# Attention and feed-forward in one kernel: shifted exponent patterns made by 64-bit additions on GpSimd, some pairs of them summed on VectorE, and an opening that gives GpSimd's work to others while a library is loaded

## The chip, the cores and the metric

The kernel runs on one core of a Trainium2 chip. The metric is the device time of one execution in microseconds (us). Three runs of the kernel before took 705.05, 705.12 and 705.44 us; the median is 705.12 us. The engines are called PE (TensorE), ACT (ScalarE), DVE (VectorE), POOL (GpSimd) and SP (SyncE, which issues most DMAs).

## The reference

With x of 2048 rows by 640, 32 heads of width 20 that share one K and one V, and a feed-forward width of 1536:

```python
xn = layernorm(x)
q = (xn @ wq) as 32 heads of 20;  k = xn @ wk;  v = xn @ wv        # k, v: 2048 x 20
A = concat_heads(softmax(q @ k.T * 20**-0.5) @ v) @ wo
B = square(relu(xn @ w1 + b1)) @ w2 + b2
out = x + A + B
```

All inputs and the output are bf16.

## The kernel before, in words

**Tiles.** The attention is cut into 32 blocks: 4 groups of 512 query rows times 8 groups of 4 heads. A block has 16 key tiles of 128 rows. A score tile is 128 keys by 512 queries of one head, so there are 32 x 16 x 4 = 2048 score tiles. One matmul of depth 20 makes one of them in a bank of PSUM (`QK..` and `DQK..`, "ps<-qT,kT" in the profile); up to four matmuls of different heads run side by side in four row groups of the array. The exponential then turns it into bf16, and a group of four matmuls, one for each head (`PV..`, `DPV..`), multiplies it with the tile of V and a column of ones and adds it up in bank 7.

**Two ways to an exponential.** ACT does the exact one: one ACTIVATE (`make_act`, L910) takes two neighbouring banks, sometimes three, into the ring `PT`. The other way is a *set*: four score tiles (the four heads) of one key tile. DVE turns each of the four into a bf16 pattern by one multiplication and addition that is written as a 16-bit integer (`D1_..`, L1083), which is a straight line in place of the exponential between powers of two. Three shifted copies of the 128x2048 pattern are made by adding 32, 64 and 96 to its 16-bit integers (`P1..P3`, the *passes*, L1101), and the four patterns go through V with the weights `TW` (0.84, 0.71, 0.59 for the shifted ones, in the tiles `vxs`), so that the four lines average to a good exponential. This takes four matmul groups in place of one. A pass runs on POOL or on DVE, by a rule in `after_dqk` that compares how far the two queues reach.

**Around it.** The rest is units of matmuls on PE with an evacuation each: transposes of xn (`unit_T`), K, V and Q, the two feed-forward layers, and the output projection. Normalising the attention goes through DRAM by DMAs that SP issues.

**The opening.** Eight DMAs on SP's queue and four on ACT's load x, wk, wv and the first columns of wq. Each group of 128 rows of x (`rows(st)`) gets its mean and variance on DVE (two BATCH_NORM_STATS2) or ACT, the inverse root on POOL (`PW..`, L434, a power of -0.5) and the normalised rows (`XN..`, L436) on DVE or POOL. PE transposes the first four groups with the identity matrix `ident` (L475), ACT moves them to SBUF (`TE..`, L477), PE makes K, Q and V of them, and the first ACTIVATE of L910 follows. POOL builds `ident` by a select (L373).

**What sets the order.** A planner in the Python of the kernel runs before the program is built. It keeps a clock for each engine, gives each operation a duration written in the code, and commits one operation after the other, by priorities that `RULES` changes for stages of 10 us. Its result is one fixed list for each engine with semaphore waits; nothing is decided on the chip. Operations marked `lock=True` (the passes, `SQ`, `CM`, `XN` and others, in SBUF alone) are planned so that one on DVE and one on POOL do not overlap, and a POOL operation of this kind waits for the last such DVE operation ahead of it. How many score tiles go each way comes out of the planner: 1480 go through ACT (665 ACTIVATEs of two, 50 of three) and 568 through 142 sets.

Of the kernel before, what the change touches and what calls it, by code (L numbers as in the profile page):

```python
# [8 lines left out]
U16 = mybir.dt.uint16  # L9
ALU = mybir.AluOpType  # L10
# [22 lines left out]
TW = [1.0, 0.83984375, 0.70703125, 0.59375]  # L33


def _pl(z):
# [17 lines left out]
JIT = 0.8  # L54
# [6 lines left out]
DLAST = 7.5  # L61
DSLACK = 0
URG = 4.0
PBIAS = 0.6
DGAP = 0.5
# [7 lines left out]
            xc=[f"FE{24 + k}" for k in range(8)] + [f"RL0_{k}" for k in range(4)] + ["RL3_0", "RL3_1", "RL3_1", "RL3_2"],  # L73
            xb=[f"RL0_{k}" for k in range(6)] + ["RL3_3", "RL3_5"])
# [4 lines left out]
ACTEV = (0, 2)  # L79
KEEP = 1  # L80
RULES = {3: {'PVA': 2.1, 'PVD': 2.1, 'R3': 1, 'PP': 0.9},
         4: {'PVA': 2.1, 'PVD': 2.1, 'R3': 1, 'PP': 0.9, 'WARM': 0.78},
         5: {'D1P': 1, 'MPRIO': 0.5, 'PBIAS': 2.5},
         6: {'D1P': 1, 'MPRIO': 0.5, 'PBIAS': 2.5, 'ND': 1, 'QKP': 0},
         7: {'DQP': 2.05, 'URG': 2, 'PVD': 2.1, 'BEHIND': -0.3},
         8: {'WARM': 0.85, 'DQP': 0.95},
         10: {'ND': 1, 'NOPEN': 3},
         11: {'ND': 1, 'NOPEN': 3},
         12: {'EPS': 0.12},
         13: {'EPS': 0.06, 'EVP': 0.3},  # L90
         15: {'PBIAS': 0},
         17: {'EPS': 0.06},
         18: {'EPS': 0.12},
         19: {'WARM': 0.78, 'PBIAS': 2.5, 'IDLE': 0.3},
         21: {'PBIAS': 0, 'KEEP': 0},
         23: {'EPS': 0.12},
         25: {'R3': 1, 'EVP': 0.3},
         26: {'R3': 1, 'EVP': 0.3, 'IDLE': 0.3, 'PVD': 2.1},
         28: {'EPS': 0.12, 'URG': 3},
         29: {'EPS': 0.12, 'URG': 3, 'KEEP': 3, 'EVP': 1.1, 'ND': 3},  # L100
         31: {'PBIAS': 1, 'D1P': 1, 'PVD': 1.05},
         32: {'PBIAS': 1, 'D1P': 1, 'PVD': 1.05, 'DGAP': 0.8, 'DQP': 0.95, 'SQP': 2, 'R3': 1},
         36: {'PP': 0.9, 'BEHIND': -0.1, 'EVP': 0.3, 'PBIAS': 1.5},
         37: {'URG': 3, 'JIT': 1.0, 'PVD': 1},
         38: {'SQP': 0.7, 'URG': 3},
         39: {'PP': 2.5},
         40: {'PBIAS': 1},
         41: {'PBIAS': 1, 'DGAP': 1.5, 'SQP': 0.7},
         42: {'PBIAS': 1, 'DGAP': 1.5, 'SQP': 2, 'NOPEN': 3, 'ND': 2, 'PVD': 1},
         43: {'PBIAS': 1, 'DGAP': 1.5, 'SQP': 2, 'NOPEN': 3, 'ND': 2, 'PVD': 1, 'R3': 9},  # L110
         44: {'WARM': 0.78, 'KEEP': 3, 'DLAST': 7.5},
         45: {'DGAP': 0.8, 'KEEP': 1, 'D1P': 3},
         48: {'PBIAS': 1},
         49: {'PBIAS': 1, 'R3': 1},
         50: {'PBIAS': 1, 'R3': 1},
         53: {'DLAST': 3.5},
         54: {'DLAST': 3.5, 'EPS': 0, 'EVP': 0.3},
         55: {'DLAST': 3.5, 'EPS': 0, 'EVP': 0.3, 'ND': 1},
         56: {'EVP': 2, 'MPRIO': 1.0},
         57: {'R3': 1, 'ND': 1},  # L120
         58: {'BEHIND': -0.1, 'EPS': 0, 'PP': 4, 'R3': 1},
         59: {'BEHIND': -0.1, 'EPS': 0, 'PP': 4, 'R3': 1, 'DRATE': 0.95, 'DLAST': 10, 'PVA': 2.1},
         60: {'EVP': 1.1},
         61: {'EVP': 1.1, 'SQP': 0.7},
         62: {'EVP': 1.1, 'SQP': 0.7, 'KEEP': 3, 'R3': 1, 'NOPEN': 2, 'D1P': 3},
         64: {'PP': 0.9, 'DRATE': 0.8},
         65: {'R3': 1},
         66: {'R3': 1},
         67: {'EPS': 0.12, 'PVA': 1.05},
         68: {'R3': 0},  # L130
         69: {'R3': 0, 'JIT': 1.1}}
HOOK = None
PRIO = {'NM15': 2.12, 'NM10': 2.88, 'PW2': 0.96}
NBEF = {'AG4': 10.21, 'NM7': 11.5, 'Qe0_1': 10.11, 'PW12': 25.33}
# [5 lines left out]
BEHIND = 0.12  # L140
IDLE = 0.3
EARLY = 12
EARLYK = "F"
FFN0 = 0.3
OUT0 = 0.5
QLEAD = 3.0
PEND = NBLK - 3.0
QCPOS = 0
ACTST = (2, 5, 6)
POOLXN = (2, 7, 9, 10, 11, 13, 14, 15)  # L150
# [9 lines left out]
                EPS=0.03, JIT=JIT, R3=R3, STATIC=STATIC, PVA=1, PVD=1, D1P=1, PP=4, SQP=2, DQP=3, QKP=0, ND=2, WARM=WARM, KEEP=KEEP)  # L160
# [64 lines left out]
def bass_parallel_sum__grouped_kv_mqa__dense_activation_squared_relu__prompt_kernel(nc, A_x, A_wq, A_wk, A_wv, A_wo, B_x, B_w1, B_b1, B_w2, B_b2, out):  # L225
    es = ExitStack()
    with es:  # L227
# [14 lines left out]
        nhalf = sb("nhalf", [128, 4], F32)  # L242
# [6 lines left out]
        vxs = sb("vxs", [128, NTERM - 1, KT, 32], BF16)  # L249
# [36 lines left out]
        fpd = nc.dram_tensor("fpd", [128, 8, HW], F32, kind="Internal").ap()  # L286
        drs = nc.dram_tensor("drs", [NBLK, 2, HPG * 512], F32, kind="Internal").ap()
# [58 lines left out]
        def op(name, eng, dur, fn, deps=(), **kw):  # L346
            o = Op(name, eng, dur, [fn], deps, **kw)
            o.prio = PRIO.get(name, o.prio)
            o.nb = NBEF.get(name, 0.0)
            ev = [d for d in o.deps if isinstance(d, str)]  # L350
            if ev:
                late.setdefault(ev[0], []).append(o)
            else:
                QUE[eng].append(o)
            return o

        def released(ev):

            for o in late.pop(ev.name, []):
                o.deps[o.deps.index(ev.name)] = ev  # L360
                QUE[o.eng].append(o)
# [4 lines left out]
        def mm(out_, l, r, start, stop, tp):  # L366
# [3 lines left out]
        c_ones = op("ones", "POOL", 0.15, lambda e: e.memset(ones_bf[:], 1.0))  # L370
        c_zero = op("zero", "POOL", 0.45, lambda e: e.memset(hT_tmp[:, 0, :], 0.0))
        c_scr = op("scr", "POOL", 0.1, lambda e: e.memset(scr[:], 1.0))
        c_id = op("ident", "POOL", 0.25, lambda e: e.affine_select(out=ident[:], in_=ones_bf[:], pattern=[[1, 128]], compare_op=ALU.is_equal,  # L373
                                                                  fill=0.0, base=0, channel_multiplier=-1), [c_ones])
        c_half = op("half", "POOL", 0.1, lambda e: e.memset(nhalf[:], -0.5))
        c_vx1 = op("vx1", "POOL", 0.12, lambda e: e.memset(vx[:, :, DH:DH + 1], 1.0))
        c_vx0 = op("vx0", "POOL", 0.25, lambda e: e.memset(vx[:, :, DH + 1:32], 0.0))
        c_z32 = op("z32", "POOL", 0.12, lambda e: e.memset(zeros32[:], 0.0))
        xv = A_x[0].rearrange("(st p) d -> p st d", p=128)
        x_op = {}  # L380
        wqv = A_wq.rearrange("(p dt) n -> p dt n", p=128)

# [5 lines left out]
        for st, land in ((0, 2.95), (1, 3.05), (2, 3.4), (3, 3.55)):  # L388
            xrows(st, st + 1, land, "ACT" if st in XACT else "SP")
        l_wk = load("wk", "ACT", lambda e: e.dma_start(wk_c[:], A_wk.rearrange("(p dt) d -> p dt d", p=128)), 4.3)  # L390
        l_wq0 = load("wq0", "SP", lambda e: e.dma_start(wq_sb[:, :, 0:80], wqv[:, :, 0:80]), 4.8)  # L391
        l_wv = load("wv", "ACT", lambda e: e.dma_start(wv_c[:], A_wv.rearrange("(p dt) d -> p dt d", p=128)), 4.8)
        for a0, a1, land in ((4, 6, 5.4), (6, 8, 5.8), (8, 12, 7.0), (12, 16, 8.5)):
            xrows(a0, a1, land)
        l_wq = load("wq", "SP", lambda e: e.dma_start(wq_sb[:, :, 80:D], wqv[:, :, 80:D]), 8.0, [HOLD["wq"]])
# [18 lines left out]

        def rows(st):
# [18 lines left out]
            pw = op(f"PW{st}", "POOL", 0.52, lambda e: e.tensor_tensor(out=rstd[:, st:st + 1], in0=mv[:, st, 1:2], in1=nhalf[:, 0:1], op=ALU.pow), [ve, c_half], lock=True, prio=st // 4)  # L434
# [4 lines left out]
        for st in range(ST):  # L439
            rows(st)  # L440

# [82 lines left out]
        def add_scaled_v(c):  # L524
            cs = slice(4 * c, 4 * c + 4)
            vs_op[c] = [op(f"VS{c}", "POOL", 0.52, lambda e, j=j: e.tensor_scalar(out=vxs[:, j - 1, cs, :], in0=vx[:, cs, :], scalar1=TW[j], scalar2=None, op0=ALU.mult), [v_op[c]], lock=True)
                        for j in range(1, NTERM)]
# [73 lines left out]
        qsem = [newctr(f"q{k}") for k in range(NQS)]  # L601
        nqc = [0]

        def unit_QC(qc, c):
# [4 lines left out]
            def evac(p, bk):  # L609
# [4 lines left out]
                for hd in range(H):  # L614
                    for cc, p0, o0, n in pieces(hd):
                        b = qc * G + hd // HPG
                        if cc == c and b > 0:
                            q_pend.append((b, k, hd % HPG, p0, o0, n, o))
# [3 lines left out]
        def q_issue():  # L622

            for x in list(q_pend):
                b, k, j, p0, o0, n, ev = x
                if b >= NQS and not blk_qk_done(b - NQS):
# [3 lines left out]
                       [ev] + (q_users.get(b - NQS, [])), lat=2.2 + DMARG, dma=qsem[b % NQS])  # L630
# [206 lines left out]
        def next_stage():  # L837
            while free["ACT"] >= stage[0] * STG:
                stage[0] += 1
                if HOOK is not None:  # L840
                    HOOK(stage[0], dict(free=free, seq=seq, late=progress() - misc[0].at if misc else 0.0))
# [7 lines left out]
        def make_step():  # L849
# [7 lines left out]
            t0 = max(free["PE"], horizon() - par("JIT"))  # L857
# [3 lines left out]
            if len(ok) >= 3 + par("R3"):  # L861
# [3 lines left out]
            if banks is None:  # L865
                can = sorted((max(st_of[bk], st_of[bk + 1], t0), bk) for bk in range(NB - 1) if st_of[bk] is not None and st_of[bk + 1] is not None)
                if not can:
                    return None
# [65 lines left out]
        def make_dpv(s, term):  # L934
            b, kt, n = s["b"], s["kt"], s["n"]
            first, last = b not in pv_begun, pv_count[b] == KT - 1 and len(s["terms"]) == 1
            src, wgt = tbuf(s["buf"][term]), (vx if term == 0 else vxs[:, term - 1, :, :])
# [6 lines left out]
            if term:  # L944
                deps.append(vs_op[kt // 4][term - 1])
# [64 lines left out]
        def lbuf_of(n):  # L1010
            return n % NL
# [447 lines left out]
```

## Time and profile before

| | |
|---|---|
| median of three runs | 705.12 us |
| span of the profiled execution, first to last instruction | 703.6 us |
| median less span | 1.5 us |
| first ACTIVATE of L910 starts | 15.30 us |
| ACT busy | 687.5 us, of it 677.1 us in the 715 ACTIVATEs of L910 |
| PE busy | 695.0 us |
| DVE busy | 645.9 us |
| POOL busy | 427.3 us, of it 395.7 us in 209 passes |
| granted clock of PE | 1.000 on average |

A row of a group reads: line, engine, operation, output and inputs with their shapes, how often (x), then the busy time of the group in us and the mean of one in ns, then the idle time of the engine just before them and what ended it. Instructions of one engine overlap a little at their ends, so a mean is longer than the distance from one start to the next, and the busy time of a group counts such an overlap once. PE's busy time is modelled and close to the span whether PE is at its peak or not.

### The profile page before, as it was taken

How to read it: one execution, taken by the hardware profiler on the slowest of the kernel's cores; microseconds unless marked ns; L12 is line 12 of the kernel's file. 1: busy time of each engine (PE TensorE's matmuls, PEld its weight loads, DVE VectorE, ACT ScalarE, POOL GpSimd, SP SyncE). 2: the span in 40 equal slices, each digit the busy share in tenths (PEclk: the TensorE clock that was granted, in tenths of full speed). 3: DMA queues.
4: the chain of work that ended last, by engine and by line, in shares of the span. 5: the costliest groups of instructions: out<-in, count | busy, mean ns of one | idle time of the engine just before them, and what ended most of it. 6: DMA issues, size and time to landing. Idle time of an engine off the chain costs nothing.

```text
span 703.6 us, 22608 instructions
## 1 busy us (share of the span) xinstructions
PE 695.0 (99%) x9780; PEld 216.0 (31%) x9781; DVE 645.9 (92%) x1125; ACT 687.5 (98%) x739; POOL 427.3 (61%) x268
## 2 busy tenths in 40 slices
PE   8999999999999999999999999999999999999997
PEld 4422223233322223332322222323333222233333
DVE  7789999999999998989998998899899999999894
ACT  6899999999999999999999999999999999999995
POOL 4767556567566764666568765766665675644253
PEclk9999999999999999999999999999999999999999
DMA  6325422233337701211101001111112100031201
GB/s 201 98 70 153 115 78 58 81 97 80 84 85 160 162 20 25 55 40 37 52 18 40 23 22 28 29 47 26 46 42 51 36 22 23 20 106 51 55 26 39
DMA packets 42016, 44.00 MB, mean 63 GB/s; under 512 B 15540, under 2 KB 32772, under 8 KB 41788
## 3 DMA queue, kind: packets, MB, share of 16 engines
q1 hardware_dynamic: 39132, 36.93, 19.2%
q0 software_dynamic: 2208, 5.25, 3.9%
q8 instruction: 76, 1.25, 0.7%
q10 hardware_dynamic: 576, 0.38, 0.2%
q14 instruction: 24, 0.20, 0.1%
HBM read 28.03 MB, written 14.91 MB: 61 GB/s over the span
## 4 chain that ended last, share of the span: by engine, by line
ACT 95%; PE 4%; DMA 1%; DVE 0%; SPq 0%; issue 0%; DVEq 0%
ACT PT L910 94%; PE ps L367 3%; DMA x_sb<-in_A_x_dram 1%; PE ps L540 1%; ACT xnT L477 0%; ACT OC L421 0%; DVE out_sb L1164 0%; PE ps L568 0%; SPq L384 0%; ACT OC L422 0%; SPq L391 0%; PE ps L510 0%; PE ps L496 0%; DVEq L227 0%; DVE PT L1164 0%
## 5 line engine op out<-in xcount | busy, mean ns | idle before, releaser
L910 ACT ACTIVATE PT<-ps 128x1024 bf16<-128x1024 f32 (+1 forms) x715 | 677.1, 1219 | 3.8 <-PE ps L367 3.8
L1083 DVE TENSOR_SCALAR tmore<-ps 128x512 uint16<-128x512 f32 x568 | 367.4, 683 | 31.7 <-PE ps L367 28.2
L1101 POOL TENSOR_SCALAR tmore<-tmore 128x2048 uint16<-128x2048 uint16 x109 | 206.4, 1900 | 171.1 <-PE ps L367 62.3
L367 PE MATMUL ps<-qT,kT 20*128 20x512 bf16 x2048 | 281.7, 384 | 1.9 <-ACT PT L910 0.8
L1101 POOL TENSOR_SCALAR x_sb<-tmore 128x2048 uint16<-128x2048 uint16 x100 | 189.3, 1902 | 79.4 <-DVE x_sb L1101 24.2
L367 PEld LDWEIGHTS ps<-qT,kT 20*128 20x128 bf16 x2048 | 71.6, 91 | 280.4 <-ACT PT L910 233.1
L367 PE MATMUL ps<-PT,vx 128*32 128x512 bf16 x1480 | 136.9, 386 | 0.2 <-ACT PT L910 0.2
L1101 DVE TENSOR_SCALAR x_sb<-tmore 128x2048 uint16<-128x2048 uint16 x135 | 96.1, 745 | 0.1
L367 PE MATMUL ps<-x_sb,vxs 128*32 128x512 bf16 x940 | 83.2, 382 | 0.0
L367 PE MATMUL ps<-xnT,w_sb 128*32 128x512 bf16 x960 | 77.2, 384 | 0.1
L367 PE MATMUL ps<-w_sb,big 128*32 128x320 bf16 x1536 | 74.5, 302 | 0.0
L367 PE MATMUL ps<-tmore,vxs 128*32 128x512 bf16 x764 | 69.6, 382 | 0.0
L1101 DVE TENSOR_SCALAR tmore<-tmore 128x2048 uint16<-128x2048 uint16 x82 | 61.5, 770 | 0.1
L367 PE MATMUL ps<-tmore,vx 128*32 128x512 bf16 x568 | 55.7, 382 | 0.0
L367 PEld LDWEIGHTS ps<-PT,vx 128*32 128x32 bf16 x1480 | 34.9, 94 | 62.1 <-issue 53.6
L367 PEld LDWEIGHTS ps<-w_sb,big 128*32 128x32 bf16 x1536 | 32.1, 95 | 29.3 <-issue 22.2
L648 DVE TENSOR_SCALAR hT_tmp<-ps,b1col 128x512 bf16<-128x512 f32 x48 | 35.8, 746 | 3.4 <-PE ps L367 2.7
L367 PE MATMUL ps<-xnT,wq_sb 128*32 128x512 bf16 (+1 forms) x480 | 33.7, 356 | 0.2 <-DVE tmore L1083 0.2
L367 PE MATMUL ps<-wo_c,OC 128*32 128x320 bf16 x608 | 30.9, 301 | 0.0
L367 PEld LDWEIGHTS ps<-x_sb,vxs 128*32 128x32 bf16 x940 | 21.3, 95 | 19.9 <-issue 13.4
L367 PEld LDWEIGHTS ps<-xnT,w_sb 128*32 128x32 bf16 x960 | 17.6, 94 | 26.7 <-issue 22.4
L367 PEld LDWEIGHTS ps<-tmore,vxs 128*32 128x32 bf16 x764 | 18.1, 95 | 16.4 <-issue 11.5
(81 smaller groups left out, 259.4 us busy)
## 6 DMA issues: line engine op xcount, KB each, us to landing
xbd<-b2d SPq DMA_DIRECT2D x16, 320.0 KB, 4.4
xbd<-in_A_x_dram POOLq DMA_DIRECT2D x8, 640.0 KB, 5.8
xr<-xbd SPq DMA_DIRECT2D x32, 160.0 KB, 2.4
w_sb<-in_B_w_dram SPq DMA_DIRECT2D x8, 480.0 KB, 4.4
big<-OR SPq DMA_DIRECT2D x71, 40.0 KB
big<-drs SPq DMA_DIRECT2D x71, 40.0 KB
out_dram<-out_sb SPq DMA_DIRECT2D x15, 160.0 KB, 1.8
qT<-QCr SPq DMA_DIRECT2D x108, 20.0 KB
```

Source lines behind the costliest of these rows:

```text
L367: return lambda e: e.matmul(out_, l, r, start=start, stop=stop, tile_position=tp)
L540: return [(lambda e, dt=dt: e.transpose(out=psbf(bk)[:, dt * 128:(dt + 1) * 128], in_=xn_sb[:, st, dt:D:DT], identity=ident[:])) for dt in ...
L648: o = Op(f"RL{qc}_{f}", "DVE", 0.66, [lambda e: e.tensor_scalar(out=hT_tmp[:, k % 2, :], in0=ps[:, bk, :], scalar1=b1col[:, f:f + 1], scal ...
L910: return Op(f"ACT{st_['j']}", "ACT", 0.05 + 0.4267 * n, [lambda e: e.activation(out=PT[:, s0:s0 + n, :], in_=ps[:, b0:b0 + (n - 1) * db + ...
L1083: d1 = op(f"D1_{n}_{i}", "DVE", 0.60, lambda e: e.tensor_scalar(out=L[:, cs].bitcast(U16), in0=ps[:, bank, :], scalar1=XA, scalar2=XB, op0 ...
L1101: p = op(f"P{j}_{n}", eng, 0.60 if eng == "DVE" else 1.86, lambda e, T=T, j=j, two=two: e.tensor_scalar(out=T.bitcast(U16), in0=L.bitcast( ...
```

## The change

1. A pass on POOL becomes one `int64_add`: the 128x2048 16-bit integers are read as 128x512 64-bit integers, and four equal shifts packed in one 64-bit number are added. The instruction belongs to a library of GpSimd that is not the standard one. The program loads the standard library as POOL's first instruction (`STD`) and the other one after the last `XN` (`LIB`); passes planned before `LIB` has ended go to DVE. The planner's duration for a pass on POOL goes from 1.86 to 1.015.
2. The weights become 1, 1, 0.707, 0.707. Pattern 0 and 1 have equal weight, and so have 2 and 3. In some sets (`ADDN` of them) DVE adds two patterns (`AD..`, one bf16 addition of 128x2048), and PE then runs one matmul group for the pair in place of two. Only one scaled tile of V is needed, made by DVE (`VS..`, 4 in place of 12 on POOL).
3. In the opening the constants are set on DVE. `ident` is made by a stair of one column of ones written to DRAM and read back with a row step of 127 (two DMAs on SP's queue, `IW` and `IR`); `IR` waits for `IW` to land. The inverse roots of the first four row groups are made together on DVE by three Newton steps of three instructions each (`NW..`), ten small instructions. `XN2` moves from POOL to DVE.
4. The planner has new parameters and a new table, may put a second step, or a single tile, beside a QK step, and evacuates the last output tiles on DVE alone (`ACTEV`). The semaphores of Q's DMAs are split in two per buffer.

What the built programs hold:

| | before | after |
|---|---|---|
| ACTIVATEs of scores, of 2 / 3 / 1 tiles | 665 / 50 / 0 | 667 / 36 / 6 |
| score tiles through ACT | 1480 | 1448 |
| sets | 142 | 150 |
| passes on POOL / on DVE | 209 / 217 | 441 / 9 |
| additions of pairs on DVE | 0 | 54 |
| matmul groups of 4 x 512 columns (with fillers) | 1281 | 1257 |
| runs of QK matmuls on PE | 714 | 683 |

```diff
-TW = [1.0, 0.83984375, 0.70703125, 0.59375]
+TW = [1.0, 1.0, 0.70703125, 0.70703125]
...
-ACTEV = (0, 2)
+ACTEV = ()
...
+PPASS = 1.015
...
-POOLXN = (2, 7, 9, 10, 11, 13, 14, 15)
+POOLXN = (7, 9, 10, 11, 13, 14, 15)
...
-        c_ones = op("ones", "POOL", 0.15, lambda e: e.memset(ones_bf[:], 1.0))
...
-        c_id = op("ident", "POOL", 0.25, lambda e: e.affine_select(out=ident[:], in_=ones_bf[:], pattern=[[1, 128]], compare_op=ALU.is_equal,
-                                                                  fill=0.0, base=0, channel_multiplier=-1), [c_ones])
...
+        std_op = op("STD", "POOL", 9.0, lambda e: e.load_library(library_config.standard))
+        c_half = op("half", "POOL", 0.1, lambda e: e.memset(nhalf[:, 0:4], -0.5))
+        c_ones = op("ones", "DVE", 0.1, lambda e: e.memset(ones_bf[:], 1.0), prio=-9)
...
+        z_ = op("idz", "DVE", 0.1, lambda e: e.memset(stair, 0.0), prio=-6)
+        o_ = op("ido", "DVE", 0.08, lambda e: e.memset(stair[:, 0:1], 1.0), [z_], prio=-5)
...
         for st, land in ((0, 2.95), (1, 3.05), (2, 3.4), (3, 3.55)):
             xrows(st, st + 1, land, "ACT" if st in XACT else "SP")
+        idw.append(load("IW", "SP", lambda e: e.dma_start(idd[0:128 * 128].rearrange("(p n) -> p n", p=128), stair), 2.2, [o_]))
...
         for a0, a1, land in ((4, 6, 5.4), (6, 8, 5.8), (8, 12, 7.0), (12, 16, 8.5)):
             xrows(a0, a1, land)
+        idd_rows = bass.AP(idd.tensor, 0, [[127, 128], [1, 128]])
+        c_id = load("IR", "SP", lambda e: e.dma_start(ident[:], idd_rows), 2.2, idw)
...
+            if st < 4:
+                pw = "NWc2"
+                ve0.append(ve)
+            else:
+                pw = op(f"PW{st}", "POOL", 0.52, ...)
...
+        nw = op("NW", "DVE", 0.1, lambda e: e.tensor_scalar(out=y4.bitcast(I32), in0=v4.bitcast(I32), scalar1=-0.5, scalar2=float(0x5f3759df), op0=ALU.mult, op1=ALU.add), ve0, prio=-1)
+        for k in range(3):
+            nw = op(f"NWa{k}", "DVE", 0.08, ...)
+            nw = op(f"NWb{k}", "DVE", 0.08, ...)
+            nw = op(f"NWc{k}", "DVE", 0.08, ...)
+        lib_op = op("LIB", "POOL", 7.5, lambda e: e.load_library(library_config.all_libraries[1]), [f"XN{st}" for st in range(ST)])
...
+            s["adds"] = min(int(add_acc[0]), 2)
+            add_acc[0] -= s["adds"]
+            if s["adds"] >= 1:
+                s["terms"].remove(0 if par("ADDB") == 0 else 3)
...
+                if lib_op.fin is None and now < lib_op_at:
+                    eng = "DVE"
+                if eng == "POOL":
+                    fn = lambda e, T=T, j=j: e.int64_add(out=T.bitcast(I64), in0=L.bitcast(I64), in1=TSTEP * j * 0x0001000100010001)
+                else:
+                    fn = lambda e, T=T, j=j: e.tensor_scalar(out=T.bitcast(U16), in0=L.bitcast(U16), scalar1=TSTEP * j, scalar2=None, op0=ALU.add)
...
+            for a, (x, y) in ((0, (0, 1)), (3, (3, 2))):
+                if a not in s["terms"]:
+                    src, dst = tbuf(s["buf"][x]), tbuf(s["buf"][y])
...
+                        p = op(f"AD{a}_{n}" ..., "DVE", 0.065 + 1.066 / ADS, lambda e, src=src[:, w], dst=dst[:, w]: e.tensor_tensor(out=dst, in0=dst, in1=src, op=ALU.add), ..., lock=True, prio=par("ADP"))
```

The constants and the table `RULES` of the planner also change throughout; they act through the orders counted above.

## The prediction

> **What bounds the kernel now.** I read the page first, then the busy time by stretches, then the forms of the groups, then the timeline of the opening. The page, on busy time, the chain that ended last, and the largest group:
>
> ```profile
> PE 695.0 (99%) x9780; PEld 216.0 (31%) x9781; DVE 645.9 (92%) x1125; ACT 687.5 (98%) x739; POOL 427.3 (61%) x268
> ACT 95%; PE 4%; DMA 1%; DVE 0%; SPq 0%; issue 0%; DVEq 0%
> L910 ACT ACTIVATE PT<-ps 128x1024 bf16<-128x1024 f32 (+1 forms) x715 | 677.1, 1219 | 3.8 <-PE ps L367 3.8
> ```
>
> The chain is ACT's, 95% of it, and the 715 exponentials waited 3.8 us in all. The table by stretches (length, then busy us of PE, PEld, DVE, ACT and POOL with instruction counts, clock, DMA) shows where:
>
> ```profile
> 0.00:15.30 15.30, 12.60 (x230) 7.03 (x231) 10.91 (x43) 9.61 (x22) 8.16 (x23) 1.00 0.67 208
> 15.30:40.00 24.70, 24.46 (x335) 10.25 (x334) 19.55 (x61) 21.96 (x23) 16.05 (x26) 1.00 0.36 103
> 200.00:360.00 160.00, 159.63 (x2214) 47.06 (x2215) 150.18 (x251) 160.00 (x171) 102.69 (x58) 1.00 0.30 68
> 520.00:695.10 175.10, 174.54 (x2545) 55.09 (x2541) 158.36 (x261) 175.10 (x179) 94.39 (x50) 1.00 0.14 39
> 695.10:703.60 8.50, 5.16 (x144) 3.44 (x136) 4.86 (x10) 0.81 (x3) 1.69 (x2) 0.97 0.22 79
> ```
>
> From 40 us to 695.1 us ACT is busy all the time. So the span is four pieces: 15.3 until the first exponential, 677.1 of exponentials, 24.70 - 21.96 = 2.7 of gaps before 40 us, 8.5 after the last. Their sum is 703.6. The median of the runs, 705.12, is 1.5 above it, and I add that 1.5 to every sum.
>
> **Fewer tiles on ACT.** 32 of 1480 tiles move to eight more sets. The forms of ACT's group:
>
> ```profile
> L910 ACT ACTIVATE PT<-ps 128x1024 bf16<-128x1024 f32 x665 | 621.9, 1190 | 1.4 <-PE ps L367 1.4
> L910 ACT ACTIVATE PT<-ps 128x1536 bf16<-128x1536 f32 x50 | 79.0, 1609 | 2.3 <-PE ps L367 2.3
> ```
>
> The third tile costs 1.609 - 1.190 = 0.419 us. With a pair at p, 665 p + 50 (p + 0.419) = 677.1, so p = 0.918, three tiles take 1.337, and one tile 0.499. After: 667 x 0.918 + 36 x 1.337 + 6 x 0.499 = 612.3 + 48.1 + 3.0 = 663.4 us, a gain of 13.7.
>
> **PE** must keep up. In the timeline near 305 us a QK run starts 0.12 us later than the group before it alone would need and holds the next back by 0.32, so a visit costs 0.43 us beyond the groups, and a group of 4 x 512 columns takes 0.216. PE loses 714 - 683 = 31 visits (13.3 us) and 24 groups (5.2 us), 18.5 together, more than ACT's 13.7. PE does not become the bound.
>
> **POOL and DVE.** The rows that price the new pass, and DVE's:
>
> ```profile
> L1101 POOL TENSOR_SCALAR tmore<-tmore 128x2048 uint16<-128x2048 uint16 x109 | 206.4, 1900 | 171.1 <-PE ps L367 62.3 <-DVE x_sb L1101 37.7 <-DVE tmore L1101 30.9
> L436 POOL TENSOR_SCALAR big<-x_sb,mv,rstd 128x640 bf16<-128x640 bf16 x8 | 7.0, 876 | 1.0 <-DVE big L436 0.5 <-DVE mv L432 0.2
> L526 POOL TENSOR_SCALAR vxs<-vx 128x128 bf16<-128x128 bf16 x12 | 6.3, 534 | 0.7
> L1083 DVE TENSOR_SCALAR tmore<-ps 128x512 uint16<-128x512 f32 x568 | 367.4, 683 | 31.7 <-PE ps L367 28.2
> L1101 DVE TENSOR_SCALAR x_sb<-tmore 128x2048 uint16<-128x2048 uint16 x135 | 96.1, 745 | 0.1
> L656 DVE TENSOR_TENSOR big<-hT_tmp 128x512 bf16<-128x512 bf16 x48 | 20.6, 445 | 0.1
> ```
>
> No row shows `int64_add`. Between 640 and 2048 elements POOL takes (1.900 - 0.876) / 1408 = 0.73 ns for each. If it counts 64-bit elements (512), the rows of 128 and 640 give 0.79 us; if 32-bit words (1024), 0.876 + 384 x 0.73 ns = 1.16 us; if packing brings nothing, 1.90. I take 1.16, since the built instruction lists its tile as 1024 32-bit words, and keep 0.79 and 1.90 as ends. 441 passes then take 512 us where 209 took 396. POOL can start them at about 43 us: its last XN ends near 31.7 before, 3 later after, and the load of the library lies behind it, priced by the planner alone at 7.5; the nine passes on DVE cover it. Until about 692 that leaves 649 us: POOL is 79% busy, under ACT.
>
> DVE loses 208 passes (of 217 in 96.1 + 61.5 = 157.6 us, so 0.73 each, 151 us) and gains 32 x 0.647 = 21 us of D1 and 54 additions. Four times the row of 512 elements gives 1.78 us for one, a pass 0.75; I take 1.4, so 76 us. DVE falls by 54 us. The ends (41 and 96) do not matter to a sum that ACT makes.
>
> **The opening.** The rows in question:
>
> ```profile
> 2.46 2.19 SPq L384 DMA_DIRECT2D x_sb<-in_A_x_dram  x4
> 7.01 0.83 PE L475 MATMUL ps<-ident,big 128*128 128x128 bf16 x10 [0.19 <-DVE big L436]
> 11.04 0.73 PE L475 MATMUL ps<-ident,big 128*128 128x128 bf16 x10
> 15.30 12.46 ACT L910 ACTIVATE PT<-ps 128x1024 bf16<-128x1024 f32 x13 [1.05 <-PE ps L367]
> x_sb<-in_A_x_dram SPq DMA_DIRECT2D x2, 640.0 KB, 7.4
> ```
>
> The inverse roots: the first four variances are there at 7.4 (the last L429 of these rows starts at 7.23), ten small instructions like L429 (0.146 us) end at 8.8, one XN later transposes could start at 9.3. That is later than 7.01 for the first pair but earlier than 11.04 for the second. The load of the standard library holds POOL, whose first `PW` comes later than at 7.4; nobody needs rows 4 to 15 before the identity is there.
>
> The identity is what I expect to be late. `IR` stands on SP's queue behind the four large loads of x, which are issued until 4.65 and land 7.4 us after issue (two of 640 KB), the last at about 12. A load of 100 KB issued at 1.72 took 5.2 us to land where the first ones of 160 KB took 2.9, so this queue serves in turn. `IR` moves little but comes last: 12.4. All four transposes, not two, then start at 12.5. From the second pair to the first exponential 4.3 us passed; two more evacuations by ACT (1.30 for two in the timeline) and half of one statistic of row 6 (0.4) come on top: 18.5. Both ends: 15.3 (identity in time) and 19.5. Everything queued behind on PE, ACT and DVE moves along; wq, held for `TE2`, comes 3 us later too, as does its user.
>
> Gaps before 40 us: 2.7 before; 0 to 4 after, I take 2.0. The tail: two evacuations of L1164 (0.42 each on DVE) come back from ACT and POOL to DVE, where eight now follow each other: 8.5 + 0.9 = 9.4. The split semaphores, `VS` and the other moves are small, beside ACT's work: nothing.
>
> **Sum:** 18.5 + 663.4 + 2.0 + 9.4 = 693.3; with 1.5, **694.8 us**.
>
> **Rivals.**
>
> *Identity in time* (chance 0.12): `IR` does not queue behind x. Against it is the 5.2 us of the small load. First exponential at 15.3: 691.6 us.
>
> *POOL answers late* (0.17): 349 matmul groups wait for POOL where 209 did. The planner reserved 1.015 us for a pass; at 1.16 a set's three end 0.43 late. PE's spare time, about 24 us for 150 sets, takes 0.16 of that; of the other 0.27 I let a fifth reach ACT, which is planned up to 0.7 us behind QK: 150 x 0.05 = 8, so 702 us. A first pass that comes some us after the library load acts the same way, once. [...]
>
> *POOL becomes the bound* (0.10), the slower side: POOL would decide from a pass of 649 / 441 = 1.47 us on. At the 1.90 of today it needs 43 + 441 x 1.90 + 10 = 891, so 892 us. For it: no row shows the instruction. Against it: 0.73 ns for each element that POOL touches, and half as many elements. [...]
>
> **Numbers.** The forecast has 0.56; 0.05 is left for stalls that I do not see. The range from 689.5 to 702.5 holds the forecast, the identity in time, and most of late POOL. A measurement here tells about 0.2% (1.4 us) from no change. Faster: 0.56 + 0.12 + 0.14 + 0.03 = 0.85. Slower: 0.10 + 0.03 of late POOL at a higher price. Same: 0.02.
>
> **What would show it.** In the profile after: L976 ACTIVATE busy near 663 with few us idle before it; the first at 18.5; transposes at L530 that wait for the DMA into `ident` until 12.5; POOL's L1181 near 1.16 mean, 441 of them near 512 us; DVE near 592. A mean over 1.47, or tens of us of PE or ACT waiting for POOL between 40 us and the end, would make the prediction wrong.

## The result

| | before | after |
|---|---|---|
| median of the runs | 705.28 us (705.05 to 705.47, 4 runs) | 697.62 us (696.73 to 701.75, 4 runs) |
| ratio | | 0.9901, 95% interval 0.9874 to 0.9928 |
| span of the profiled execution | 703.6 us | 695.6 us |
| first exponential starts | 15.30 us | 22.05 us |
| the exponentials | 677.1 us | 663.3 us |
| gaps between them before 42 us | 2.7 us (before 40 us) | 1.4 us |
| after the last one | 8.5 us | 8.9 us |

The four pieces account for the 8.0 us between the two spans: +6.75 - 13.8 - 1.3 + 0.4. The runs of the kernel after lie further apart than those of before, and the granted clock of PE goes with them: 0.995 on average in the run of 696.73 us, 0.988 in the one of 701.75.

The page of the kernel after, on busy time, the largest group, the passes on POOL, the first group of additions on DVE, and the chain:

```profile
PE 678.3 (98%) x9683; PEld 214.6 (31%) x9685; DVE 606.7 (87%) x1028; ACT 673.4 (97%) x731; POOL 471.5 (68%) x474
ACT 92%; PE 5%; DMA 1%; SPq 0%; DVE 0%; issue 0%; DVEq 0%
L976 ACT ACTIVATE PT<-ps 128x1024 bf16<-128x1024 f32 (+1 forms) x709 | 663.3, 1216 | 2.4 <-PE ps L402 2.4
L1181 POOL INT64_ADD x_sb<-tmore x245 | 252.2, 1045 | 70.8 <-DVE tmore L1195 21.7
L1181 POOL INT64_ADD tmore<-tmore x196 | 201.3, 1041 | 115.7 <-DVE big L710 39.9
L1195 DVE TENSOR_TENSOR tmore<-tmore 128x2048 bf16<-128x2048 bf16 x37 | 47.0, 1273 | 0.0
```

ACT's share of the chain went from 95% to 92%, but its exponentials still waited only 2.4 us in all: ACT remains the bound, with less work. A pass on POOL takes 1.04 us.

The table by stretches of the kernel after (length, then busy us of PE, PEld, DVE, ACT and POOL with counts, clock, DMA share, GB/s):

```profile
5.50:12.50 7.00, 0.00 (x0) 0.00 (x1) 6.21 (x26) 2.50 (x6) 0.69 (x2) 0.64 0.76 260
12.50:15.00 2.50, 2.47 (x21) 2.17 (x21) 0.00 (x0) 1.73 (x3) 0.00 (x0) 0.50 0.00 0
15.00:17.00 2.00, 2.00 (x63) 1.58 (x66) 1.04 (x5) 1.03 (x3) 0.00 (x0) 0.50 0.23 20
17.00:18.00 1.00, 1.00 (x37) 0.77 (x29) 0.68 (x4) 0.10 (x1) 0.14 (x1) 0.62 0.91 301
22.05:42.00 19.95, 19.02 (x250) 8.43 (x250) 17.14 (x64) 18.58 (x22) 11.74 (x17) 1.00 0.37 103
200.00:360.00 160.00, 159.49 (x2293) 48.92 (x2293) 143.52 (x224) 160.00 (x172) 113.00 (x110) 1.00 0.20 49
520.00:686.70 166.70, 164.57 (x2337) 49.89 (x2333) 146.19 (x231) 166.70 (x178) 123.37 (x121) 1.00 0.14 38
686.70:695.60 8.90, 5.55 (x152) 3.76 (x148) 5.65 (x12) 0.03 (x1) 0.00 (x0) 1.00 0.21 76
```

From 42 us to the last exponential ACT has no idle time, as before. The news is in the first four rows: PE does nothing for 7.0 us, and its granted clock, which was 1.00 through all of the opening before, falls to 0.50 and stays there until about 17.7 us. Four moments of that time, and POOL's first passes, in the timeline (start, length, then engine and instruction, with the idle time before it and what ended it):

```profile
5.12 0.60 SPq L435 DMA_DIRECT2D ident<-idd  x1
8.86 0.09 POOL L406 MEMSET nhalf<- 128x4 f32 x1 [8.42 <-issue]
9.43 1.52 DVE L483 TENSOR_SCALAR big<-x_sb,mv,rstd 128x640 bf16<-128x640 bf16 x4
12.53 2.30 PE L530 MATMUL ps<-ident,big 128*128 128x128 bf16 x20 [7.09 <-DMA ident<-idd]
22.05 2.86 ACT L976 ACTIVATE PT<-ps 128x1024 bf16<-128x1024 f32 x3 [1.06 <-PE ps L402]
...
55.92 2.06 POOL L1181 INT64_ADD tmore<-tmore  x2 [16.26 <-DVE big L710]
```

The rows of x are normalised from 9.43 us on; the identity lands at 12.4 us, 7.3 us after its issue, and the twenty transposes take 2.30 us where two times ten took 0.83 + 0.73 in the kernel before. The load of the standard library holds POOL for 8.42 us. The other library's load lies in the 16.26 us ahead of POOL's first pass, which was waiting for DVE when it started.

### The profile page after: what moved, and what is told of

It is laid out like the page before. It is cut to its first block, busy times and chain, and to the rows that moved or that the text cites. A ratio compares the mean times of both kernels' runs of the same rounds, so it can differ in the third digit from the quotient of the medians.

```text
span 695.6 us, 22438 instructions
## 1 busy us (share of the span) xinstructions
PE 678.3 (98%) x9683; PEld 214.6 (31%) x9685; DVE 606.7 (87%) x1028; ACT 673.4 (97%) x731; POOL 471.5 (68%) x474
## 4 chain that ended last, share of the span: by engine, by line
ACT 92%; PE 5%; DMA 1%; SPq 0%; DVE 0%; issue 0%; DVEq 0%
ACT PT L976 92%; PE ps L402 4%; DMA ident<-idd 1%; PE ps L594 1%; PE ps L530 0%; SPq L422 0%; DVE out_sb L1256 0%; PE ps L622 0%; PE ps L565 0%; PE ps L551 0%; SPq L430 0%; DVE PT L1256 0%; DVEq L253 0%; SPq L428 0%; DVE hT_tmp L408 0%
## 5 line engine op out<-in xcount | busy, mean ns | idle before, releaser
L976 ACT ACTIVATE PT<-ps 128x1024 bf16<-128x1024 f32 (+1 forms) x709 | 663.3, 1216 | 2.4 <-PE ps L402 2.4
L1161 DVE TENSOR_SCALAR tmore<-ps 128x512 uint16<-128x512 f32 x600 | 390.9, 685 | 49.0 <-PE ps L402 43.2
L1181 POOL INT64_ADD x_sb<-tmore x245 | 252.2, 1045 | 70.8 <-DVE tmore L1195 21.7
L1181 POOL INT64_ADD tmore<-tmore x196 | 201.3, 1041 | 115.7 <-DVE big L710 39.9
L402 PE MATMUL ps<-qT,kT 20*128 20x512 bf16 x2048 | 269.9, 384 | 2.6 <-ACT PT L976 1.6
L402 PE MATMUL ps<-tmore,vx 128*32 128x512 bf16 x796 | 73.3, 383 | 0.0
L1195 DVE TENSOR_TENSOR tmore<-tmore 128x2048 bf16<-128x2048 bf16 x37 | 47.0, 1273 | 0.0
L402 PE MATMUL ps<-tmore,vxs 128*32 128x512 bf16 x396 | 35.7, 382 | 0.0
L402 PEld LDWEIGHTS ps<-tmore,vx 128*32 128x32 bf16 x796 | 19.3, 95 | 20.0 <-issue 13.4
L1044 DVE COPY OR<-ps 128x512 f32<-128x512 f32 x30 | 20.6, 685 | 2.3 <-PE ps L402 1.9
```

The source lines that it names most:

```text
L402: return lambda e: e.matmul(out_, l, r, start=start, stop=stop, tile_position=tp)
L976: return Op(f"ACT{st_['j']}", "ACT", 0.05 + 0.4267 * n, [lambda e: e.activation(out=PT[:, s0:s0 + n, :], in_=ps[:, b0:b0 + (n - 1) * db + ...
L1044: tn = op(f"TN{b}", "DVE", 0.60, lambda e: e.tensor_copy(out=OR[:, a, :], in_=ps[:, PVB, :]), [lastpv] + or_users[a], prio=0)
L1161: d1 = op(f"D1_{n}_{i}", "DVE", 0.60, lambda e: e.tensor_scalar(out=L[:, cs].bitcast(U16), in0=ps[:, bank, :], scalar1=XA, scalar2=XB, op0 ...
L1181: fn = lambda e, T=T, j=j: e.int64_add(out=T.bitcast(I64), in0=L.bitcast(I64), in1=TSTEP * j * 0x0001000100010001)
L1195: p = op(f"AD{a}_{n}" if q == ADS - 1 else f"AE{a}_{n}_{q}", "DVE", 0.065 + 1.066 / ADS, lambda e, src=src[:, w], dst=dst[:, w]: e.tensor_ ...
```

## The experiments

Unless something else is said, an experiment is the kernel after with one edit, made behind the planner, so that the rest of the order stays.

### The opening: what is late, and why the first exponential was 3.5 us later than forecast

**The identity on another queue**

```diff
+ir = next(o for o in order_all if o.name == "IR")
+ir.eng = "ACT"            # SP before; now behind the loads of x on ACT's queue
```

> The DMA that reads the identity back goes from SP's queue, where it stands behind all of x, to ACT's queue, issued at about 6.3 us; all else keeps its order. The theory: in the changed kernel the first exponential starts at 22.05 us, not at 18.5, because the identity comes at 12.5 us and because PE, idle from 5.5 us on, is granted half its clock from about 7.5 to 17.6 us. Then here the transposes start at about 9.9 us (the first normalised rows at 9.43 + 0.44 decide), still on half the clock, the first exponential starts at about 19.4, and the median falls by 2.6 us to 695.0. Rival 1, the lateness alone (the clock does not matter): 22.05 - 2.6 as well, so this run does not part them, but the next two do. Rival 2, the statistics of rows 4 to 15 on DVE set the pace until 40 us: the first exponential comes earlier, the gaps after it grow by as much, and the median stays at 697.6.

Measured: 700.93 us as the median of three runs (697.47 to 701.94; a fourth, at a clock of 0.971, took 709.23), ratio 0.9914 (0.9882 to 0.9946), so no gain on 697.62. How long the small DMA took, in the kernel after and here, and one stretch of the opening here:

```profile
ident<-idd SPq DMA_DIRECT2D x1, 32.0 KB, 7.3
ident<-idd ACTq DMA_DIRECT2D x1, 32.0 KB, 5.9
```

```profile
22.50:27.50 5.00, 5.00 (x25) 1.59 (x27) 4.13 (x16) 4.12 (x6) 2.89 (x5) 0.50 0.38 105
```

Without the large loads ahead of it in its own queue it still took 5.9 us, and landed at 11.4 us instead of 12.4. So waiting in turn behind x on SP's queue, which is how the prediction explained it, is worth only about 1 us. The rest fits DMA engines that are all taken by x: in the kernel after their mean busy share is 1.02 between 8 and 9 us. The transposes started at 11.54 us, still at half clock, and the clock fell a second time at about 22 us, so that the gaps between exponentials before 50 us came to 5.3 us, where the kernel after has 1.4.

**PE kept busy while it waits**

```diff
+t0 = next(k for k, o in enumerate(order_all) if o.name == "T0")
+order_all[t0:t0] = [Op("fill", "PE", 0.215, warm_parts(), [c_ones, c_zero]) for _ in range(30)]
```

> 30 filler matmuls more on PE ahead of the first transpose, so that PE is busy while it waits for the identity; the identity stays late. The theory of the clock: the granted clock stays at 1.0, the 20 transposes take about 1.5 us and not 2.30, a group of 20 small matmuls 0.46 and not 0.71, the first exponential starts at about 18.5 us (the number of the prediction) and the median falls by 3.5 us to 694.1. Rival 1 (the clock costs nothing, ACT's order or DVE make the chain): the first exponential stays near 22 and the median at 697.6. Rival 2 (rows 4 to 15): first exponential near 18.5, gaps before 40 us 3.5 larger, the median near 697.6. The runs should also lie closer together than the 696.7 to 701.8 of the changed kernel if the cold clock made that spread.

Measured: 696.89 us (694.67 to 699.01), ratio 0.9868 (0.9835 to 0.9901). The waiting stretch, and the transposes and the first exponential in the timeline:

```profile
5.50:12.50 7.00, 7.00 (x32) 3.13 (x31) 6.08 (x26) 2.57 (x6) 0.69 (x2) 1.00 0.76 267
```

```profile
12.72 1.28 PE L530 MATMUL ps<-ident,big 128*128 128x128 bf16 x20
...
19.19 5.61 ACT L976 ACTIVATE PT<-ps 128x1024 bf16<-128x1024 f32 x6
```

With filler matmuls the clock stays at 1.00, the transposes take 1.28 us instead of 2.30, and the first exponential starts at 19.19 us with the identity no earlier than before. That is 2.9 of the 3.5 us by which the forecast missed it. The profiled execution took 694.67 us. But only two of four runs kept the clock for the whole of their time (1.000, 694.67 and 694.88 us); the others had 0.993 on average and 698.9 and 699.0 us. So the main cause of the late first exponential is shown, and the median has not moved for certain: 4.1 us go with 0.007 of the mean clock, lost at a place that the runs without a profile do not show.

**Both**

```diff
+ir.eng = "ACT"
+order_all[t0:t0] = [Op("fill", ...) for _ in range(18)]
```

> Both edits: the identity by ACT's queue, and 18 filler matmuls more, which reach to about 9.5 us. The theory: transposes at about 9.9 us on the full clock, first exponential at about 15.9 us, median 697.6 - 6.1 = 691.5. If both edits add up, the lateness and the clock are the whole of what the opening lost against the kernel before (first exponential at 15.30). Rival (rows 4 to 15 on DVE decide until 40 us): about 695 or more, with gaps of 4 us or more between the first exponential and 40 us.

Measured: 697.71 us (693.47 to 698.40), ratio 0.9885 (0.9868 to 0.9901). The profiled execution, at a clock of 1.000, has its first exponential at 18.07 us and takes 693.47 us; the other four, at 0.992 to 0.995, take 696.8 to 698.4. The first exponential is 2.2 us later than the 15.9 expected: the transposes wait for the identity until 11.23 us, not 9.9, and from there to the first exponential 6.8 us pass at the full clock, not 6.0.

**The standard library loaded at the end of the execution before**

```diff
-(IW and IR: identity through DRAM)
+ir.eng, ir.deps = "POOL", [c_ones]                # identity by a select, as before
+ir.parts = [lambda e: e.affine_select(out=ident[:], in_=ones_bf[:], ...)]
+order_all.append(Op("END", "POOL", 0.0, [lambda e: e.load_library(library_config.standard)]))
```

> The program loads the standard library once more as POOL's last instruction, so that the next execution finds it there, and POOL makes the identity again by a select right after the load at the start; the two DMAs for the identity are left out. If a load of the library that is already there is free (in the kernel before, the load ahead of the select left no gap), the 8.4 us that POOL waits at the start fall to under 0.5, the identity is there at about 1.5 us, the transposes start at about 9.9 us (the normalised rows decide), PE's clock still falls to half, and the first exponential starts near 19.4; time about 695. If every load costs its 8 us, POOL waits 8.4 us as now, the identity comes at about 9.3 us, and the transposes start at about the same time, 9.9. The load at the end lies beside the tail of 8.9 us: 0 to 3 us longer.

Measured: 699.9 us (one run). POOL's first instructions behind the load at the start:

```profile
1.15 0.29 POOL L1499 TENSOR_SCALAR_AFFINE_SELECT ident<-OR 128x128 bf16<-128x128 bf16 x1 [0.64 <-DVE OR L407]
1.40 0.10 POOL L406 MEMSET nhalf<- 128x4 f32 x1
```

The program still loads the standard library first, but where that library is in place already the load costs nothing that can be seen: `nhalf` is set at 1.40 us instead of 8.86. (The execution before has left it there, by the load at its end; a first execution behind another program was not measured.) The transposes moved to 10.08 us, again at half clock, the first exponential to 19.43, and then the clock fell a second time between 20 and 30 us, with gaps of 5.8 us (1.4 in the kernel after). What the earlier start had won (2.6 us) was lost there.

### The passes on POOL: what a late pass costs

**Every fourth pass done twice**

```diff
+passes = [o for o in order_all if o.eng == "POOL" and o.name[0] == "P" and o.name[1] in "123"]
+for o in passes[::4]:
+    x = Op(o.name + "x", "POOL", 0.0, o.parts, o.deps)
+    order_all.insert(order_all.index(o), x)
+    o.deps = o.deps + [x]
```

> Every fourth pass on POOL is done twice (110 more `int64_add`, each pair one after the other); nothing else changes. A pass then costs 1.045 x 1.25 = 1.31 us on average, 576 us in all, of the 631 us between the first pass (55.9) and the last (687). The theory (ACT sets the pace from 42 us on, POOL's passes lie beside it, under the point of 1.43 us a pass): the ACTIVATEs of scores keep under 1 us of waiting after 42 us, and the time stays at the changed kernel's, 697 to 698, give or take the 2 us of its opening. The rival of the prediction (late POOL): passes that end late hold PE, and PE holds ACT; at 0.05 us for each of 150 sets 705, at 0.1 us 712, and the waits stand in the ACT row after 42 us.

Measured: 798.69 us as the median of three runs (789.82 to 798.87; a fourth, at the lowest clock, 0.902, took 805.30), ratio 1.1251 (1.1172 to 1.1330). Neither my theory nor the rival's price is near. The 552 passes that ran are 111 more than the 441, and cost 101 us, with POOL busy 611 of 797 us. Its waits (us in total, times, longest):

```profile
ACT PT L976 <- PE ps L402: 83.5, 132, 2.9
PEld ps L402 <- POOL x_sb L1181: 40.7, 60, 2.3
PE ps L402 <- POOL x_sb L1181: 22.7, 30, 2.0
```

and two of its stretches:

```profile
226.00:250.00 24.00, 22.95 (x290) 6.08 (x286) 22.22 (x36) 23.32 (x26) 20.37 (x21) 1.00 0.46 98
110.00:140.00 30.00, 28.23 (x292) 7.25 (x284) 17.57 (x27) 20.51 (x21) 19.78 (x19) 0.63 0.25 72
```

PE waits for a late pass, ACT waits for PE. Where the clock stays up, ACT loses 0.7 of 24 us. Where it has fallen to a mean of 0.63, PE is busy 28.2 of 30 us, and ACT loses 9.5. At the rate of the run with fillers (4.1 us for 0.007) the fall of the mean clock from 0.993 to 0.916 would be some 45 of the 101 us; this division is an estimate.

**The 16-bit pass of the kernel before, in the new order**

```diff
-fn = ... e.int64_add(out=T.bitcast(I64), in0=L.bitcast(I64), in1=TSTEP * j * 0x0001000100010001)
+fn = ... e.tensor_scalar(out=T.bitcast(U16), in0=L.bitcast(U16), scalar1=TSTEP * j, scalar2=1.0, op0=ALU.add, op1=ALU.mult)
```

> The passes on POOL are again the 16-bit additions of the kernel before, in the changed kernel's order (the library is still loaded, and not used). POOL needs 441 x 1.90 = 838 us. The theory: POOL becomes the bound, 55.9 + 838 + 10 = 904 us of span, and ACT waits some 200 us for PE, which waits for POOL. If the passes were not worth their price (the order would hide them either way), the time would stay under 720.

Measured: 1045.34 us (one run). The larger group of passes and the clock in forty slices, from its page:

```profile
PEclk8996567685657978685969856757886795667858
L1181 POOL TENSOR_SCALAR x_sb<-tmore 128x2048 uint16<-128x2048 uint16 x245 | 479.0, 1982 | 45.8 <-DVE tmore L1195 14.2
```

POOL is busy 873 of 1043 us, so it is not even full: it holds PE up (between 60 and 780 us, 43.5 + 27.1 us of PE's waits end with a pass), PE's mean clock is down to 0.738, and ACT stands idle for 306 us between its exponentials. Pricing a slow POOL by its busy time alone (a span of 904 us) was 139 us short of the 1043. So the 64-bit instruction is what makes this order possible: 1.04 us against 1.98.

**Every pass a quarter longer**

The base of this run and of the next is the version with a better opening that comes last in this section (692.71 us).

```diff
-fn = lambda e: e.int64_add(out=T.bitcast(I64), ...)
+fn = [lambda e, w=w: e.int64_add(out=T[:, w].bitcast(I64), ...) for w in (first half, second half)]
```

> On the opening of the run with 20 fillers (692.71 us), each of the 441 additions on GpSimd is issued as two, each over half of the columns. I put one pair at about 1.2 us against 1.04 for the whole, near the 1.16 that the prediction took: 441 x 0.15 = 66 us more on GpSimd, to about 520 of 693. Theory of the prediction: GpSimd still has room, so the longer passes are hidden: 693 to 695 us. Rival, from the run with every fourth pass done twice (110 x about 1.1 us more on GpSimd cost 101 us): what GpSimd loses is passed on nearly in full, 66 x 0.85 = 56 us, about 749 us.

Measured: 728.81 us as the median of three runs (724.41 to 730.49; a fourth, at the lowest clock, 0.967, took 736.46), ratio 1.0311 (1.0269 to 1.0353); 36.1 us over its base. The passes of the base, then those of this run:

```profile
L1181 POOL INT64_ADD x_sb<-tmore x245 | 253.0, 1049 | 70.3 <-DVE tmore L1195 21.7
L1181 POOL INT64_ADD tmore<-tmore x196 | 201.7, 1043 | 115.1 <-DVE big L710 39.7
```

```profile
L1181 POOL INT64_ADD x_sb<-tmore x490 | 313.5, 667 | 38.4 <-PE ps L402 10.7
L1181 POOL INT64_ADD tmore<-tmore x392 | 248.4, 662 | 77.7 <-DVE big L710 31.6
```

561.9 us for 441 passes is 1.27 us each: 0.24 more than the 454.7 us of the base, not the 0.15 I had put down. So about a third of what POOL loses (36.1 of 107 us) reaches the end: not hidden, and not passed on in full. ACT stands idle for 28 us after 42 us, and 18 of them lie in three stretches of 50 us (from 150, 450 and 650 us on) whose mean clock is 0.97, 0.83 and 0.97. One place shows how. PE in the timeline, then the stretch behind it:

```profile
470.10 0.40 PE L402 MATMUL ps<-tmore,vx 128*32 128x512 bf16 x4 [0.24 <-POOL tmore L1181]
472.24 0.40 PE L402 MATMUL ps<-x_sb,vxs 128*32 128x512 bf16 x4 [1.74 <-POOL x_sb L1181]
```

```profile
474.00:475.00 1.00, 1.00 (x18) 0.38 (x14) 0.00 (x0) 0.75 (x2) 1.00 (x2) 0.65 0.00 0
479.00:492.00 13.00, 13.00 (x133) 3.62 (x134) 7.00 (x12) 8.19 (x8) 4.99 (x9) 0.52 0.15 40
```

PE waits 1.74 us for a pass, about 2 us later its clock is at half, and until 492 us ACT is busy only 8.19 of 13 us.

**Every sixteenth pass done twice**

```diff
-for o in passes[::4]:
+for o in passes[::16]:
```

> On the opening of the run with 20 fillers (692.71 us), every 16th pass on GpSimd is done twice: 28 passes more, 29 us, each a single delay of 1.04 us. Theory: single delays of a microsecond are taken up by the buffers: 693 to 694.5 us. Rival, in proportion to the run with every fourth pass done twice (110 more passes, 101 us more): 28 x 0.92 = 26 us, about 718 us.

Measured: 701.97 us (701.40 to 710.23), ratio 0.9940 (0.9923 to 0.9956). Three of its five runs have a clock of 0.999, with 701.4 to 702.0 us: their median is 9.1 us over the base, 0.32 us for each of the 28 passes added, with no loss of clock to speak of. So a single delay isn't absorbed either; that PE's order has too little behind a late pass would explain it, but was not tested. A delay is also more than the pass itself: in the profiled execution the passes took 496.2 us, 41.5 more than in the base and not 29, and 30 of the 54 additions on DVE overlapped a pass, against 17 in the base. The two other runs, at 0.992 and 0.985, took 705.8 and 710.2 us.

### The pairs summed on DVE

```diff
-ADDN = 0.5                (and the entries ADDN of RULES)
+ADDN = 0                  (the planner then makes 144 sets, and 1472 tiles go through ACT)
```

Once on the kernel after, once on the version with the better opening:

> The planner runs with ADDN = 0 everywhere: no pair is summed on DVE, and it then finds room for 144 sets instead of 150, so 1472 score tiles go through ACT (664 ACTIVATEs of two, 46 of three, 6 of one). The passes stay 64-bit additions, the opening the same. The theory (the time is ACT's sum): 664 x 0.918 + 46 x 1.337 + 6 x 0.499 = 674.1 us of ACT, 10.8 more than the changed kernel's 663.3, so 708 us: the 64-bit passes alone, with this opening, would be no faster than the kernel before, and the pairs, by the PE time that they free, are what buys the gain. The rival (the faster passes are the gain, pairs matter little): about 699.

> On the opening of the run with 20 fillers (692.71 us), no pair is summed on VectorE: ScalarE passes over 1472 tiles in place of the pair sums, 674.1 us of exponentials against 663.3. Theory: ScalarE is full from 42 us to the end, so the pairs are worth what they take off ScalarE, 10.8 us: 703.5 us. Rival: the pairs only move waiting from one place to another, and without them the time is 693 to 695 us.

Measured: 713.66 us on the kernel after (ratio 1.0093, 1.0063 to 1.0122), with a clock of 0.984 to 0.986 in four of five runs and 708.55 us at 0.995 in the fifth; the profiled one lost 5.6 us in gaps of the opening. On the other opening, where the clock held (0.998 to 1.000), 704.15 us (703.71 to 704.48, nine runs; 0.9973, 0.9963 to 0.9982). Its exponentials:

```profile
L976 ACT ACTIVATE PT<-ps 128x1024 bf16<-128x1024 f32 (+1 forms) x716 | 674.8, 1205 | 3.1 <-PE ps L402 2.9
```

Against 692.71 that is 11.4 us; 10.8 had been worked out from the tile prices of the prediction. The pairs take matmul groups off PE, which lets the planner make six more sets, and so they take 24 tiles off ACT. Without them, even with the better opening, the kernel is only 0.3% faster than before.

### A better opening

```diff
+(the library loaded at the end, identity on POOL: as above)
-(NW..: inverse roots of the first four row groups on DVE)
+new.append(Op(f"PW{st}", "POOL", 0.52, [... pow ...], [ve0[st], c_half]))
+(10 fillers before T0; fillers before K2 1, QK0 1, QK1 2, T6.0 3, QK2 1, QK3 1, QK4 1)
```

> The standard library is loaded once more at the end; the identity (a select) and the inverse roots of the first four row groups are POOL's again, as in the kernel before; and PE gets 20 more filler matmuls, ten ahead of the first transpose and ten in the gaps up to the fifth QK step. The theory: the roots are there at about 8.0 us, the transposes start at 8.0 on a clock of 1.0, the first exponential starts at 14.9, and with gaps of 2 us before 42 us the time is 697.6 - 7.1 = 690.5, in every run, since the clock no longer drops. The rival (rows 4 to 15 on DVE and POOL decide until 42 us): the gaps before 42 us grow by what the first exponential gained, about 694; and if fillers do not hold the clock, the runs spread over 4 us as before.

Measured: 692.71 us (692.22 to 693.23), ratio 0.9811 (0.9795 to 0.9828). Its timeline:

```profile
1.16 0.29 POOL L1499 TENSOR_SCALAR_AFFINE_SELECT ident<-OR 128x128 bf16<-128x128 bf16 x1 [0.65 <-DVE OR L407]
8.96 1.28 PE L530 MATMUL ps<-ident,big 128*128 128x128 bf16 x20
15.98 1.94 ACT L976 ACTIVATE PT<-ps 128x1024 bf16<-128x1024 f32 x2 [0.52 <-PE ps L402]
```

The first exponential starts 6.1 us earlier than in the kernel after, 2.3 us of gaps follow (1.4 there), and the clock is 0.999 or 1.000 in all four runs, which lie within 1.0 us of each other. Its four pieces are 15.98 + 663.8 + 2.3 + 8.9 = 691.0, the span. Nearly all of what the opening of the kernel after had cost against the one before (15.30 us) is back, with the fewer tiles kept. The 690.5 us expected were missed by 2.2: the transposes start at 8.96 us, behind the last filler, not at 8.0, and the first exponential is 1.1 us later than expected.

The same with 6 fillers before `T0` and 5 in the gaps:

> The run with library, identity and roots rearranged and 20 filler matmuls (median 692.71 us) is taken again with 11 fillers: 6 instead of 10 ahead of the transposes, 5 instead of 10 in the gaps up to the last opening group. My theory: the fillers ahead of the transposes only have to bridge the time until the clock would fall, so six do as well, and the first exponential comes up to 1 us earlier (15.0 to 16.0 us): 691.3 to 692.7 us. Rival: the fillers in the gaps are what holds the clock; with fewer the granted clock falls again in some runs, the median is 695 or more and the runs spread over 3 us or more.

Measured: 692.00 us (691.47 to 694.96), ratio 0.9811 (0.9787 to 0.9834). Three runs, at a clock of 0.998 to 1.000, took 691.5 to 692.2 us. The profiled execution has its transposes at 7.78 us and its first exponential at 15.11, but lost its clock near the end, after PE had been idle for 0.12, 0.21 and 0.52 us of three successive microseconds:

```profile
664.00:676.00 12.00, 11.48 (x93) 2.25 (x93) 6.41 (x11) 8.68 (x9) 7.05 (x8) 0.57 0.01 1
```

ACT loses 3.3 us there. With four runs each the two versions can't be told apart; both beat the kernel before by about 1.9% and the kernel after by about 0.8%.

## Why the prediction came out as it did

694.8 us were forecast and 697.62 measured, in the range. On the profiled execution, the sum without the 1.5 us (693.3) and the span (695.6) differ by 2.3 us, and the pieces are these; the other 0.5 is that the median lies 2.0 us above the span, not 1.5.

**The first exponential, 18.5 against 22.05: the term that was mis-sized.** The late identity was right to a tenth (12.4; the transposes started at 12.53). What failed is the step behind it: "from the second pair to the first exponential 4.3 us passed" was read from an opening in which PE, once started, never waited more than 0.52 us and ran at full clock (1.00). The step moved this work behind 7 us of idle PE, and did not ask what the idle time does to PE. The fillers show that the clock is 2.9 of the 3.5 us. The other 0.7 is left at the full clock: from the transposes to the first exponential 6.5 us pass there, where the sum had 6.0. In the kernel after the clock fell to 0.50 2.1 us after PE's last matmul of the warm-up, and it came back 5.2 us after the first transpose. The reason given for the late identity was only partly right: on ACT's queue, with x not ahead of it, it was still 5.9 us under way. The ten small instructions for the inverse roots took 1.9 us (7.45 to 9.39), not 1.5, which the late identity hid.

**The exponentials, 663.4 against 663.3.** The prices of two, three and one tile from the rows of before held, and so did the reading that ACT is full from 42 us on. The gaps (1.4, taken 2.0) and the tail (8.9, taken 9.4) gave 1.1 us back.

**POOL.** A pass costs 1.04 us, between the ends of 0.79 and 1.90, below the 1.16 taken; 453.5 us in all, not 512. The first one starts at 55.92 us, not at 43: DVE makes the first pattern between 49.45 and 52.9 us, and by the profile the pass then still waits for another operation of DVE (L710). ACT has no gap in that time. The planner's 1.015 was met to within 0.03, so POOL answers in time.

**The price of a late POOL was too low, and the error did not show.** The prediction let a fifth of what PE cannot cover reach ACT: at its own 1.16 us this gave 8 us, as a rival, and nothing in the sum. For the pass of 1.27 us the same working gives 3 x 0.26 - 0.16 = 0.62 us a set, a fifth of it 0.12, and 19 us in 150 sets; measured were 36.1, twice as much. So 1.16 us would have cost some 16 us by the same correction (an estimate), and the forecast at its own price ought to have been near 711. A pass taken too long and a consequence left out cancelled each other, so that the forecast lies in the range is in part luck. The rival *POOL becomes the bound* had the same flaw: by its working a pass of 1.98 us gives 43 + 441 x 1.98 + 10 + 1.5 = 928 us, and 1045 were measured, at a mean clock of 0.738. Its break-even of 1.47 us is too high as well: at 1.27 the time (728.8) is already past that of the kernel before.

**DVE and PE.** An addition takes 1.28 us (taken 1.4). The durations of DVE's instructions add up to 54 us less than before (667.6 against 721.7), as forecast, though its busy time, which counts overlapping ends once, fell by 39 only, to 607 and not to 592. PE did not become the bound.

## What to carry to other kernels

Work that is moved behind a wait of PE must be priced at the clock that PE has after the wait (here 0.50, behind 7.09 us without a matmul), and not with the durations of an opening in which its longest wait was 0.52 us; useless matmuls in the gap can be the cover: here 30 of them kept the clock of the opening at 1.00, and the twenty transposes took 1.28 us in place of 2.30. When an engine's answer is planned to within some hundredths of a microsecond, its busy share says little about the cost of being late: at 80% busy, a pass of 1.27 us instead of 1.03 cost 5% of the time. And where runs of one kernel lie apart, look at the mean clock of each before comparing medians: here it was 0.995 in the run of 696.73 us and 0.988 in the one of 701.75.

## What the runs showed of the hardware

- **A fall of the clock can follow a small wait and costs more than it.** PE idle for 1.74 us in the run with split passes was followed by about 18 us at half clock, and ACT lost 8.3 us between 468 and 492 us. In the run with 11 fillers the 0.85 us of idle time between 662 and 665 us came ahead of a fall at 665 us; in the run with every sixteenth pass doubled, 0.92 us at 668 us did not bring it down at once; it fell at 676 us, behind 0.77 us of idle time between 673 and 676 us. That the fall follows from idle time is shown for the opening alone (with fillers the clock of the waiting stretch is 1.00, without them it falls to 0.50); what amount of idle time decides in the middle of a run stays open.
- **A second fall between 20 and 34 us**, with PE then busy without a break at half speed (5.00 of 5.00 us in the first two, 4.00 of 4.00 in the third, clock 0.50), brought three of the profiled openings to gaps of 5.3 to 5.8 us (identity on ACT's queue, library at the end, no pairs). In the first of them PE had been idle for 1.9 us between 19 and 22 us; in the kernel after, where no second fall came, for 0.8 between 18 and 22. In the two versions with fillers in the gaps as well it did not come either, but neither did it in the profiled executions with fillers ahead of the transposes alone, so that the fillers in the gaps are what prevents it is not shown.
- **Loading a GpSimd library** that is in place already costs nothing visible (POOL sets `nhalf` at 1.40 us in the run with the library loaded at the end, at 8.86 in the kernel after); the same load held POOL for 8.42 us where another one was in place. POOL's first two passes behind the other load took 2.06 us together, with a mean of 1.04 us for all passes.
- **DVE's addition takes longer beside a pass on POOL.** In the kernel after, 38 of the 54 additions overlap no pass (by more than 0.15 us) and take 1.21 us; the other 16 take 1.45. Of the 17 passes that an addition overlaps, 16 take 1.03 to 1.05 us (the 424 others 1.04 on average), and one, at 313.06 us, takes 2.00. With every sixteenth pass doubled, 30 overlap one and take 1.69. With every fourth pass doubled, in the timeline:

```profile
150.00 5.23 POOL L1181 INT64_ADD tmore<-tmore  x5
...
154.24 2.06 DVE L1195 TENSOR_TENSOR tmore<-tmore 128x2048 bf16<-128x2048 bf16 x1 [1.43 <-POOL tmore L1181]
```

The addition starts 0.99 us before the last pass ends, and takes 0.99 + 1.07 us: as if it had begun only then. What makes it wait is not shown.
